# Blockwise causal attention and a max-of-two MLP: w_out asked for one slot later, one k copy on ScalarE, early y copies on VectorE, score bursts further apart, last y tile in three PSUM tiles

## The chip, the cores and the metric

The kernel runs on one core of a Trainium2 chip. The metric is the device time of one execution in microseconds (us). TensorE does the matmuls, VectorE (DVE), ScalarE (ACT) and GpSimd (POOL) the rest; SP only issues transfers. "PEld" is TensorE's weight load.

## The reference, cut to what matters

```python
def _attn_ref(q, k, v):                    # q, k, v: (8, 8, 576, 64) float32
    scores = scale * np.matmul(q, k.transpose(0, 1, 3, 2))
    ...                                    # causal by blocks of 64: block_i >= block_j
    attn = np.exp(scores - max); attn = attn / sum
    return np.matmul(attn, v)

def _moe_ref(x, w1, w2, w_out):            # x: attention output as (4608, 512)
    g = np.maximum(x @ w1, x @ w2)         # w1, w2: 512 x 1024
    return g @ w_out                       # w_out: 1024 x 512
```

## The kernel before

The program is one hand-made schedule. Two heads make a pair, and 32 pairs make 32 "slots": slot s computes the scores and exps of pair s in two bursts, then the attention-times-v matmuls of pair s - 2. The matmuls of the MLP (units "h" for w1 and w2, units "y" for w_out) are strewn between as filler, as soon as their tokens are done. q and k arrive in groups of two pairs: a load on the SP queue, a cast to bfloat16 on GpSimd, 18 small transposes on TensorE and two copies, for q and for k each. v and the weights come through GpSimd's queue, which casts on the way.

```python
def y_unit(i, s):                          # one 128 x 512 tile of the output
    ...
        if f == NFF - 1:
            y = y_pool.tile([P, d_model], FP32, name="y")
            nc.scalar.copy(out=y[:], in_=py[:])
            nc.sync.dma_start(out=out[t0:t0 + P, :], in_=y[:])

def pool_work(s):                          # GpSimd's work of slot s
    g, i = divmod(s, 2)
    if s == 4:
        pass
    elif s == 5:
        load_qk(5, (SP, SP), gated=True)
        cast("q", 4, ((pool, 0, RPP),))
    ...

# before the loop over slots (slot 3)
burst_q1(3)
transposes("k", 2, (dve, dve))()
...
cast("q", 3, ((pool, 0, RPP),))
cast("k", 3, ((pool, 0, RPP),))
load_qk(4, (SP, SP), gated=True)           # q and k group 4, used from slot 6 on
load_wo(0, 4)
load_wo(4, 4)
...
for s in range(HP, NPAIR):                 # slots 4 to 31
    n = fill_of(s)                         # filler of this slot
    burst_a(s)
    n_a = n // 2 if n > 12 else n * 2 // 5
    fill(n_a)                              # filler between the two bursts
    copy_out = t_pair(s)                   # transposes of a later group
    burst_b(s)
    ...
```

The PSUM pool of everything but scores has four buffers, in rotation. "Gated" loads are those whose place in time GpSimd sets: it writes one element of the buffer first.

The softmax here doesn't subtract the row's maximum and nothing guards it: scores larger than these inputs give would overflow.

## Time and profile before

| | before |
|---|---|
| time, median of 3 runs | 291.29 us |
| span of the profiled run | 289.4 us |
| TensorE busy | 280.3 us, 97% |
| VectorE, ScalarE, GpSimd busy | 64%, 48%, 35% |
| transfers from 22 to 48 us | the 16 DMA engines never idle |

Busy shares say that TensorE is the bound. They do not say where it waits, and only there can this change win. The useful reading is a list of gaps between neighbouring matmuls, each with what ended it. The prediction below gives it, with the lines of the timelines and of the chain of waits.

Wherever the kind of matmul changes between full 128-row and half 64-row form, the gap is about 0.095 us more than the steady step. The Trainium skill, "TensorEngine Tiling (Array Packing)", section "Key Properties", says that changing the tiling mode drains TensorE. The traces fit this and give the price. Such gaps are not waits, and no part of this change touches them.

### The profile page before, as it was taken

The numbers are of one execution on the slowest core, as the hardware profiler recorded it, in microseconds if no ns is written. First come the engines' busy times: TensorE is split into PE (matmuls) and PEld (weight loads), VectorE is DVE, ScalarE is ACT, GpSimd is POOL, SyncE is SP. The second block draws the span as 40 slices with busy tenths as digits, with TensorE's granted clock in tenths as the row PEclk, the third lists the DMA queues.
The fourth block names the chain that finished last, engine by engine and source line by source line (L and its number), as shares of the span: only waits on it lengthen the run. The fifth ranks groups of instructions, "written<-read, shape, count | busy, mean of one in ns | idle before, by whom it ended". The sixth has DMA issues, their size and how long they took to land.

```text
span 289.4 us, 7674 instructions
## 1 busy us (share of the span) xinstructions
PE 280.3 (97%) x3200; PEld 145.2 (50%) x3200; DVE 186.2 (64%) x391; ACT 137.8 (48%) x196; POOL 101.2 (35%) x241
## 2 busy tenths in 40 slices
PE   7799989999999999999999999999999999999995
PEld 3356556555554554544454545454454554444443
DVE  6878778548986676666566656567665766545430
ACT  3785755786555555554555554545555110010112
POOL 2978547335635442244334532543111000000000
PEclk9999999999999999999999999999999999999999
DMA  7999999969933792569366593366201011111114
GB/s 265 237 219 276 172 286 216 182 166 165 198 48 134 96 214 49 198 76 228 57 202 70 157 132 99 112 69 72 48 36 39 36 39 72 40 57 52 57 55 145
DMA packets 56083, 36.68 MB, mean 127 GB/s; under 512 B 38768, under 2 KB 43376, under 8 KB 56048
## 3 DMA queue, kind: packets, MB, share of 16 engines
q0 software_dynamic: 41728, 7.87, 33.8%
q1 hardware_dynamic: 13760, 27.60, 28.2%
q10 hardware_dynamic: 560, 0.72, 0.7%
q8 instruction: 25, 0.41, 0.6%
q14 instruction: 10, 0.08, 0.1%
HBM read 34.60 MB, written 9.44 MB: 152 GB/s over the span
## 4 chain that ended last, share of the span: by engine, by line
PE 88%; DMA 4%; issue 2%; DVE 2%; ACT 2%; POOL 1%; ACTq 0%; POOLq 0%; DVEq 0%
PE ps_h L191 41%; PE ps_y L209 21%; PE ps_o L396 12%; PE ps_s L318 8%; DMA vv<-in_v_dram 2%; PE ps_xe L418 2%; DMA qraw<-in_q_dram 2%; PE ps_qT L301 2%; PE ps_kT L301 1%; ACT aT L324 1%; PE ps_w L290 1%; DVE xp L403 1%; POOL vv L130 1%; PE ps_y L226 1%; POOL qn L126 1%
## 5 line engine op out<-in xcount | busy, mean ns | idle before, releaser
L191 PE MATMUL ps_h<-xT,w_sb 128*128 128x512 bf16 (+3 forms) x640 | 140.7, 358 | 0.4 <-DVE kT L308 0.2
L324 ACT ACTIVATE aT<-ps_s 128x1024 bf16<-128x1024 f32 (+3 forms) x128 | 100.1, 832 | 60.4 <-PE ps_s L318 58.5
L191 PEld LDWEIGHTS <-w_sb 128*128 128x128 bf16 x640 | 56.8, 98 | 57.1 <-issue 6.1
L198 DVE CAST h<-ps_h 128x512 bf16<-128x512 f32 (+3 forms) x80 | 50.9, 636 | 43.4 <-PE ps_h L191 41.2
L209 PE MATMUL ps_y<-wo_sb,g 128*128 128x512 bf16 x280 | 69.4, 379 | 0.0
L329 POOL MEMSET aT<- 64x128 bf16 x122 | 22.6, 201 | 110.3 <-ACT aT L324 110.0
L215 ACT COPY y<-ps_y 128x512 f32<-128x512 f32 x35 | 20.5, 587 | 81.8 <-PE ps_y L209 59.3
L200 DVE TENSOR_TENSOR g<-h,ps_h 128x512 bf16<-128x512 bf16 (+3 forms) x80 | 50.6, 632 | 9.9 <-PE ps_h L191 7.6
L396 PEld LDWEIGHTS <-aT 128*128 128x128 bf16 x960 | 34.0, 98 | 14.6 <-DVE xp L403 7.2
L396 PE MATMUL ps_o<-vv,aT 128*128 128x65 bf16 x960 | 40.2, 194 | 0.5 <-DMA vv<-in_v_dram 0.4
L209 PEld LDWEIGHTS <-g 128*128 128x128 bf16 x280 | 25.5, 98 | 27.4 <-issue 3.0
L318 PE MATMUL ps_s<-qT,kT 64*128 64x64 bf16 (+6 forms) x408 | 34.7, 269 | 1.3 <-ACT kT L308 0.7
L130 POOL DMA_DIRECT2D vv<-in_v_dram x40 | 33.7, 849 | 0.0
L403 DVE TENSOR_TENSOR xp<-ps_o,rec 128x256 bf16<-128x256 f32 (+1 forms) x64 | 31.4, 491 | 2.2
L318 PEld LDWEIGHTS <-kT 64*128 64x128 bf16 x408 | 16.2, 94 | 15.4 <-issue 9.7
L402 DVE RECIPROCAL rec<-ps_o 128x4 f32<-128x4 f32 (+1 forms) x64 | 11.8, 185 | 14.6 <-PE ps_o L396 14.5
L126 POOL CAST qn<-qraw 128x1152 bf16<-128x1152 f32 (+1 forms) x15 | 16.5, 1102 | 6.9 <-DMA qraw<-in_q_dram 6.7
L126 POOL CAST kn<-kraw 128x1152 bf16<-128x1152 f32 x15 | 17.2, 1145 | 4.1 <-DMA kraw<-in_k_dram 2.0
L181 POOL COPY g<-g 128x512 bf16<-128x512 bf16 x8 | 4.9, 614 | 37.9 <-DVE g L200 37.8
L308 DVE COPY qT<-ps_qT 128x576 bf16<-128x576 bf16 x18 | 13.5, 757 | 5.5 <-PE ps_qT L301 4.6
L308 DVE COPY kT<-ps_kT 128x576 bf16<-128x576 bf16 x18 | 13.5, 755 | 3.9 <-PE ps_kT L301 2.8
L423 DVE COPY xT<-ps_xe 128x640 bf16<-128x640 bf16 (+2 forms) x18 | 8.2, 453 | 11.9 <-PE ps_xe L418 11.4
(40 smaller groups left out, 110.9 us busy)
## 6 DMA issues: line engine op xcount, KB each, us to landing
qraw<-in_q_dram SPq DMA_DIRECT2D x16, 576.0 KB, 4.5
out_dram<-y SPq DMA_DIRECT2D x35, 256.0 KB, 2.1
kraw<-in_k_dram SPq DMA_DIRECT2D x15, 576.0 KB, 6.3
vv<-in_v_dram POOLq DMA_DIRECT2D x32, 128.0 KB, 5.6
w_sb<-in_moe_w_dram POOLq DMA_DIRECT2D x4, 256.0 KB, 6.5
w_sb<-in_moe_w_dram POOLq DMA_DIRECT2D x2, 512.0 KB, 14.2
wo_sb<-in_moe_w_out_dram POOLq DMA_DIRECT2D x2, 512.0 KB, 16.0
kraw<-in_k_dram ACTq DMA_DIRECT2D x1, 576.0 KB, 5.4
```

What stands on the lines that cost most here:

```text
L126: copy(out=n[:, j0:j1], in_=t[:, j0:j1])
L130: nc.gpsimd.dma_start(out=vv_r[b % NV][:rows, c, :, :D], in_=v[b, :, c * P:c * P + rows, :].rearrange("h p d -> p h d"),)
L191: nc.tensor.matmul(pt[:, :w], w_sb[:, c, f * P:(f + 1) * P], xT[:, c, t0:t0 + w], start=(c == 0), stop=(c == NDM - 1),)
L198: nc.vector.tensor_copy(out=h1[:, :w], in_=pt[:, :w])
L200: nc.vector.tensor_max(g[:, f, m:m + w], h1[:, :w], pt[:, :w])
L209: nc.tensor.matmul(py[:], g[:, f, s * P:(s + 1) * P], wo_sb[:, f, :], start=(f == 0), stop=(f == NFF - 1),)
L308: copies[i](out=t[:, :S].rearrange("q (p j) -> q p j", j=RPP), in_=pts[i].rearrange("q j p -> q p j"),)
L318: nc.tensor.matmul(ps[:m, hh, col:col + w], kT[r, c * P:c * P + m], qT[r, q0:q0 + w], start=True, stop=True,)
L324: nc.scalar.activation(out=aT_r[p % NA][:m, :, a0:a0 + w], in_=ps[:m, :, :w], func=AF.Exp, scale=scale,)
L329: (eng or nc.gpsimd).memset(aT_r[p % NA][BLK:, :, a0:a0 + BLK], 0.0)
L396: nc.tensor.matmul(po[:, gi, hh, :], a[:, hh, a0:a0 + P], vv[:, c, h0 + 2 * hh, :], start=(mm == 0), stop=(mm == n_mm - 1),)
L403: nc.vector.tensor_mul(xp[:, ts[0]:ts[0] + n, :, p % 2], po[:, :, :, :D], rec[:, :n].to_broadcast([P, n, 2, D]),)
```

## The change

Its intent: w_out's megabyte should not compete with the load of q group 4; ScalarE, which has the exps, should not have y copies in front of them; VectorE, busy in slot 3, should give one k copy to ScalarE; the filler of slot 4 should cover the wait for its exp; the two halves of the last tile's copy should not wait for each other.

```diff
--- before.py
+++ after.py
@@ -212,28 +212,24 @@
             )
             if f == NFF - 1:
                 y = y_pool.tile([P, d_model], FP32, name="y")
-                nc.scalar.copy(out=y[:], in_=py[:])
+                (dve if i < 2 else act)(out=y[:], in_=py[:])
                 nc.sync.dma_start(out=out[t0:t0 + P, :], in_=y[:])
             yield
 
     def y_last(i, s):
         g = g_tiles[i]
         t0 = spans[i][0] - carry[i] + s * P
-        w = d_model // 2
-        for h in range(2):
+        for m, w, copy, queue in ((0, 256, act, SP), (256, P, dve, SP), (384, P, act, ACT)):
             py = ps_m.tile([P, w], FP32, name="ps_y", tag="m")
             for f in range(NFF):
                 nc.tensor.matmul(
-                    py[:], g[:, f, s * P:(s + 1) * P], wo_sb[:, f, h * w:(h + 1) * w],
+                    py[:], g[:, f, s * P:(s + 1) * P], wo_sb[:, f, m:m + w],
                     start=(f == 0), stop=(f == NFF - 1),
                 )
                 if f == NFF - 1:
-                    for u, (copy, queue) in enumerate(((act, ACT), (dve, SP))):
-                        m = u * w // 2
-                        y = y_pool.tile([P, w // 2], FP32, name="yl")
-                        copy(out=y[:], in_=py[:, m:m + w // 2])
-                        queue.dma_start(
-                            out=out[t0:t0 + P, h * w + m:h * w + m + w // 2], in_=y[:])
+                    y = y_pool.tile([P, w], FP32, name="yl")
+                    copy(out=y[:], in_=py[:])
+                    queue.dma_start(out=out[t0:t0 + P, m:m + w], in_=y[:])
                 yield
 
 
@@ -247,7 +243,7 @@
         def y(i, s, last=False):
             t0, w = spans[i]
             if last:
-                units.append((y_last(i, s), t0 + w, 0.5, 2 * NFF))
+                units.append((y_last(i, s), t0 + w, 0.333, 3 * NFF))
             else:
                 units.append((y_unit(i, s), t0 + w, 1.0, NFF))
 
@@ -440,7 +436,8 @@
     def pool_work(s):
         g, i = divmod(s, 2)
         if s == 4:
-            pass
+            load_wo(0, 4)
+            load_wo(4, 4)
         elif s == 5:
             load_qk(5, (SP, SP), gated=True)
             cast("q", 4, ((pool, 0, RPP),))
@@ -527,7 +524,7 @@
         load_v(1, c)
     fill(3)
     burst_q1(3)
-    transposes("k", 2, (dve, dve))()
+    transposes("k", 2, (dve, act))()
     av(0, [3, 4])
     fill(3)
     burst_q2(3)
@@ -535,8 +532,6 @@
     cast("q", 3, ((pool, 0, RPP),))
     cast("k", 3, ((pool, 0, RPP),))
     load_qk(4, (SP, SP), gated=True)
-    load_wo(0, 4)
-    load_wo(4, 4)
     fill(3)
     av(1, [3, 4])
     fill(4)
@@ -548,7 +543,7 @@
             x_out(x_due.pop(), 3 if s < HP + 2 else 0)
         n = fill_of(s)
         burst_a(s)
-        n_a = n // 2 if n > 12 else n * 2 // 5
+        n_a = n // 2 if n > 12 else n * 3 // 5
         n_b = n // 6
         fill(n_a)
         copy_out = t_pair(s)
```

## The prediction

> **What bounds the kernel now.** I read the page first, then the gaps between matmuls, then what ended each gap. The page says TensorE is busy for 97% of the span and its clock is fully granted, and the chain of waits agrees:
>
> ```profile
> span 289.4 us, 7674 instructions
> PE 280.3 (97%) x3200; PEld 145.2 (50%) x3200; DVE 186.2 (64%) x391; ACT 137.8 (48%) x196; POOL 101.2 (35%) x241
> ...
> PE 88%; DMA 4%; issue 2%; DVE 2%; ACT 2%; POOL 1%; ACTq 0%; POOLq 0%; DVEq 0%
> ```
>
> So a change that adds no faster matmul can win only where TensorE waits. I looked for those places by subtracting, for each pair of neighbouring matmuls, the steady step of the first kind (0.2155 us for 512 columns, 0.162 for 384, 0.030 for an attention-times-v matmul) from the distance of their starts. A change of matmul kind costs about 0.095 us everywhere; beyond that, from 70 us to 210 us no gap exceeds 0.125 us. The change touches only what lies before 66 us and after 284 us. In those parts the real waits are these. In slot 4: about 0.09 us at 26.7, 0.68 us at 28.9 (scores wait for an exp) and 0.15 us at 31.4. In slot 6: 1.00 us before the transposes of q group 4. From 46.6 to 50.4: about 1.3 us in which VectorE is behind. In slot 9: 0.19 us at 59.1. The large one, in the timelines of TensorE, GpSimd and the SP queue:
>
> ```profile
> 40.12 0.44 PE L301 MATMUL ps_qT<-ident,qn 64*128 64x64 bf16 x18 [0.93 <-POOL qn L126]
> ...
> 30.38 1.50 POOL L144 DMA_DIRECT2D wo_sb<-in_moe_w_out_dram  x2
> 31.92 0.64 POOL L329 MEMSET aT<- 64x128 bf16 x4
> ...
> 38.92 1.14 POOL L126 CAST qn<-qraw 128x1152 bf16<-128x1152 f32 x1 [2.20 <-DMA qraw<-in_q_dram]
> ...
> 30.44 0.37 SPq L116 DMA_DIRECT2D qraw<-in_q_dram  x1
> ```
>
> TensorE waits for a cast, the cast waits for a load of q, and that load was issued at 30.44, 0.06 us after the two w_out loads began to be issued. The view of the transfers, for issues near 30.4 us, gives how long they took:
>
> ```profile
> qraw<-in_q_dram SPq DMA_DIRECT2D x1, 576.0 KB, 8.4
> wo_sb<-in_moe_w_out_dram POOLq DMA_DIRECT2D x1, 512.0 KB, 14.6
> ```
>
> The median load of q takes 4.5 us, this one 8.4. It looks as if w_out were in its way; that is plainly the intent of the first part of the change.
>
> The other two places, in the chain:
>
> ```profile
> 58.88 0.49 ACT y L215
> ...
> 284.48 1.76 PE ps_y L226 x16
> 286.24 0.02 issue
> 286.26 0.28 ACT yl L234
> 286.54 0.02 issue
> 286.56 0.29 DVE yl L234
> ```
>
> In slot 9 a y copy sits behind two exps on ScalarE, and its PSUM buffer is what the next attention matmuls need. At the end, VectorE's copy of the last quarter starts only when ScalarE's has ended, and the last store (1.6 us to landing) is issued after both.
>
> **What the Trainium skill says.** "DMA: Bandwidth & Descriptors", section "Queues, rings and completion order", says each of the 16 engines serves its queues in turn, packet by packet, and takes one queue's work in ring order. The trace agrees: while the q load and w_out run together (37.0 to 39.5 us) each half microsecond has about 45 packets of the SP queue and 40 of GpSimd's; and w_out, issued from 30.38, has its first packet only at 35.5, when nearly all of the v loads issued before it on that queue are through. "PSUM — Partial Sum Buffer", section "PSUM bank collisions raise a hardware error", says two engines may not use one bank's partitions at once, so software orders them; the ScalarE-then-VectorE order of the last tile in the chain shows just that. "VectorE: DVE Perf Modes", "Why PSUM operands drop a tier", says a float32 source in PSUM runs at the base rate; the 128x512 casts here take 691 ns against ScalarE's 587 ns for a y copy.
>
> **Part by part.**
>
> 1. *w_out later.* The order of GpSimd's instructions shows what "one slot" is: the two loads move behind the four masks of slot 4. Those masks took 0.64 us once GpSimd was free, and slot 4's third exp, which the last needs, ends at about 30.5. So the loads start at about 31.0 instead of 30.38: 0.6 us, not the six of a slot. And they stand in their ring behind v packets, which last to about 35.5 on most engines, so the first w_out packet should hardly move. The packet records also show the completion marks of this q load: fifteen of its sixteen came by 37.98, the last at 38.56, and until 39.4 a thin trickle of v packets (about 18 per us, one ring's worth) goes on. I read that as one lagging engine, where v and q alternate and w_out has not begun. Delaying w_out cannot help that engine much. I put the gain at 0.15 us: zero most likely, up to the whole 1.0 us if I misread the laggard. w_out itself landed at 45.0 and 48.5; 0.6 us later is still 3 us before its first use at 52.1.
>
> 2. *k copy on ScalarE* (slot 3) takes 0.71 us off VectorE, which is busy 1.86 of the two microseconds from 24 to 26; ScalarE is idle for 0.79 us there. It lets the x transposes at 27.0 start 0.09 us sooner.
>
> 3. *Bursts further apart* changes one slot only: in slot 4 four h matmuls instead of three stand before the second burst. They fill 0.16 us of the 0.68 us wait for the exp.
>
> Parts 2 and 3 together give 0.25 us, but before 38.9 us, where TensorE stands still for q anyway. The load's time does not depend on them: its issue is set by the k load before it (issued 18.16, 10.9 us to landing, so 29.06; its cast starts at 29.22). They only lengthen the wait from 1.00 to 1.25 us. Worth 0, unless q lands sooner.
>
> 4. *Early y copies on VectorE*: four tiles at about 0.69 us (the 128x512 cast row). The one at 58.76 can now start when its matmuls end, 58.0, because VectorE is idle for 2.8 us before 59.07; the buffer is free at 58.7, before the attention matmuls want it at 59.2. Gain 0.19 us. The other three fall after attention work in slots 8 to 10 with VectorE idle 2.81, 0.69 and 1.81 us around them: free.
>
> 5. *Last tile in three.* Eight matmuls of 256 columns become 16 of 128. From the steps seen (0.110 us for 256, 0.083 for 192) a 128-column one takes about 0.056, so TensorE takes 0.88 + 16 x 0.056 = 1.78 us, 0.02 more. After its end only one copy (0.27 us) remains instead of ScalarE's and VectorE's (0.28 + 0.02 + 0.29). The final store then goes out at 286.58 instead of 286.87. Gain 0.29 - 0.02 = 0.27 us.
>
> Sum: 0.15 + 0 + 0.19 + 0.27 = 0.61 us. 291.29 - 0.6 = 290.7 us.
>
> **Rivals.**
> - *w_out really was what delayed q.* For it: they share engines from 35.5 to 38.9, in which some 250 w_out packets of 97 ns pass, 250 x 97 / 16 = 1.5 us of every engine. Against: ring order keeps w_out where it is, and 0.6 us of delay is little. If true, q lands up to 1 us sooner, and parts 2 and 3 pay as well: 1.0 to 1.25 us more, 289.5.
> - *The wait moves to v.* The last v load of batch 1 lands at 25.6 + 14.6 = 40.2 us and is needed at 41.4. If q came over a microsecond sooner, this would be the next wait; it caps the first rival, not the estimate.
> - *VectorE becomes the bound.* From 46.6 to 50.4 it holds TensorE up, but the y copies begin only at 54.7, after that. If a copy landed before a kT or qT copy it could cost 0.3 us: 291.0.
> - *Later w_out or other packet order makes q or k land later.* GpSimd builds w_out's descriptors just after 31 us, when the k load is being issued on SP (1.35 us there, against 0.42 elsewhere). A shift by half a microsecond either way: 291.3.
>
> **Range and chances.** Copies and tail are firm to about 0.15 us. The q load is the wide term: most likely 0, with a tail to 1.0-1.25 us of gain and a thinner one to 0.5 us of loss. So 290.7, eight in ten from 289.6 to 291.2. 2% is 5.8 us, more than all the waits touched together; faster 0.01, same 0.98, slower 0.01.
>
> **What would show it.** GpSimd's issue of w_out near 31.0, its first packets still near 35.5, and the cast of q still starting between 38.7 and 39.0 with a TensorE wait of 1.0 to 1.3 us before its transposes (step 1 to 3); if the cast starts before 38.5, the ring-order argument is wrong. No gap over 0.1 us before the attention matmuls in slot 9 (step 4). One copy after the last matmul and about 0.29 us less from there to the end (step 5). The middle, 70 to 210 us, must keep its length; a change there would mean I missed something.

## The result, and the profile after

In the same rounds the changed kernel took 290.90 us (median of 4 runs, 290.44 to 290.96) and the kernel before 291.45 us (4 runs, 291.25 to 291.81). The ratio is 0.9976, with a 95% interval of 0.9959 to 0.9994.

Page of the changed kernel, its first lines and the chain by engine:

```profile
span 289.0 us, 7689 instructions
PE 280.2 (97%) x3208; PEld 145.4 (50%) x3208; DVE 187.9 (65%) x393; ACT 136.4 (47%) x193; POOL 101.0 (35%) x241
...
PE 89%; DMA 4%; issue 2%; DVE 2%; POOL 1%; ACT 1%; ACTq 0%; POOLq 0%; DVEq 0%
```

Nothing has changed in kind: eight more matmuls, the same bound. Now the place where TensorE waits for q. Timelines of the changed kernel for TensorE, GpSimd and SP; columns are start, duration, engine, line, operation, and in brackets the idle time before it and what ended that:

```profile
40.02 0.44 PE L297 MATMUL ps_qT<-ident,qn 64*128 64x64 bf16 x18 [0.96 <-POOL qn L126]
...
30.58 0.62 POOL L325 MEMSET aT<- 64x128 bf16 x4
31.15 1.50 POOL L144 DMA_DIRECT2D wo_sb<-in_moe_w_out_dram  x2
...
38.83 1.14 POOL L126 CAST qn<-qraw 128x1152 bf16<-128x1152 f32 x1 [2.23 <-DMA qraw<-in_q_dram]
...
30.51 0.37 SPq L116 DMA_DIRECT2D qraw<-in_q_dram  x1
```

The masks and the w_out loads have changed places, w_out's issue is 0.77 us later (31.15 against 30.38), and the cast of q still begins at 38.83 (38.92 before). The view of the transfers says the same of the load itself:

```profile
qraw<-in_q_dram SPq DMA_DIRECT2D x1, 576.0 KB, 8.3
```

8.3 us to landing, 8.4 before. In slot 9 the y copy is gone from the chain of the changed kernel:

```profile
58.57 0.37 PE ps_kT L297 x18
58.94 0.25 PE ps_s L314 x6
59.19 0.29 PE ps_o L392 x6
```

The attention matmuls follow the scores at once. At the end the chain has one copy where it had two:

```profile
284.23 1.78 PE ps_y L225 x24
286.01 0.02 issue
286.03 0.27 ACT yl L231
```

To see where the time went I cut each profiled run at the same instructions: from the k transposes of group 2 (slot 3) to the moment when TensorE is ready for q group 4; the wait for q there; from q group 5's transposes to q group 6's (holds slot 9); from the last q transposes to the end.

| profiled run | to ready for q4 | wait for q4 | slot 9 stretch | to the end |
|---|---|---|---|---|
| before | 16.37 | 1.00 | 11.33 | 91.39 |
| after | 16.28 | 1.03 | 11.19 | 91.19 |
| difference | -0.09 | +0.03 | -0.14 | -0.20 |

All numbers are in us. The rest agrees: from q group 4's transposes to group 5's 13.15 in both, from group 6's to the last q transposes 133.44 and 133.43. So 0.34 us is won after q has come (0.14 + 0.20), and what is won before is at the mercy of a load.

### The profile page after: what moved, and what is told of

Read it like the earlier page. It is cut to its first block, busy times and chain, and to the rows that moved or that the text cites. A ratio compares the mean times of both kernels' runs of the same rounds, so it can differ in the third digit from the quotient of the medians.

```text
span 289.0 us, 7689 instructions
## 1 busy us (share of the span) xinstructions
PE 280.2 (97%) x3208; PEld 145.4 (50%) x3208; DVE 187.9 (65%) x393; ACT 136.4 (47%) x193; POOL 101.0 (35%) x241
## 4 chain that ended last, share of the span: by engine, by line
PE 89%; DMA 4%; issue 2%; DVE 2%; POOL 1%; ACT 1%; ACTq 0%; POOLq 0%; DVEq 0%
PE ps_h L191 41%; PE ps_y L209 21%; PE ps_o L392 12%; PE ps_s L314 8%; DMA vv<-in_v_dram 2%; PE ps_xe L414 2%; DMA qraw<-in_q_dram 2%; PE ps_qT L297 2%; PE ps_kT L297 2%; PE ps_w L286 1%; ACT aT L320 1%; DVE xp L399 1%; POOL vv L130 1%; PE ps_y L225 1%; POOL qn L126 1%
## 5 line engine op out<-in xcount | busy, mean ns | idle before, releaser
L215 ACT COPY y<-ps_y 128x512 f32<-128x512 f32 x31 | 18.1, 585 | 81.3 <-PE ps_y L209 58.8
L304 DVE COPY kT<-ps_kT 128x576 bf16<-128x576 bf16 x17 | 12.8, 755 | 1.4 <-PE ps_kT L297 0.3
```

The lines of the kernel that those rows point to most:

```text
L304: copies[i](out=t[:, :S].rearrange("q (p j) -> q p j", j=RPP), in_=pts[i].rearrange("q j p -> q p j"),)
```

## The experiments

Twelve kernels in three groups of four, five rounds each; the kernels of a group share the runs of the kernel before, and the second and third group have eleven of these in common. Times are medians. A transfer moves in many small packets. "Marks" are the sixteen increments of a semaphore that make up a landing, read here as one from each of the 16 DMA engines; both are in the trace's records.

### Each part alone

**w_out_only**: the kernel before with this edit.

```diff
-    load_wo(0, 4)            # before the loop
-    load_wo(4, 4)
...
     if s == 4:
-        pass
+        load_wo(0, 4)
+        load_wo(4, 4)
```

> The kernel before with the w_out loads alone moved into slot 4. Theory (ring order and one lagging engine): the issue moves from 30.4 to about 31.1 us, the cast of q group 4 still starts at 38.7 to 39.0, the time is that of before within 0.15 us (ratio 0.9995 to 1.0005). Rival (w_out held q up): the cast starts before 38.4 and the time falls by 0.5 us or more (ratio under 0.9985).

Measured: 291.30 us (6 runs, 290.26 to 291.83) against 291.51 (11 runs, 291.02 to 292.02); ratio 0.9986, interval 0.9970 to 1.0002. In the profile w_out is issued at 30.70, its first packet comes at 35.95 (35.74 before), and the cast of q starts at 38.26, where the theory had 38.7 to 39.0 and the rival less than 38.4: the first half of the rival's sign. But q itself was issued 0.37 us sooner in that run (30.07), and took 8.14 us from issue to landing against 8.43. The clock leans towards a gain but its interval holds zero.

**y_copies_only**: the kernel before with `(dve if i < 2 else act)` for the y copy.

> The kernel before with the first four y copies alone on VectorE. Theory: the 0.19 us wait before the attention matmuls of slot 9 goes and all that follows comes that much sooner, 0.2 us less (ratio about 0.9993). Rival (VectorE becomes the bound in slots 8 to 10): a new gap before a kT or qT copy's reader, no gain or up to 0.3 us lost.

Measured: 291.19 us (6 runs, 291.08 to 291.89), ratio 0.9993, interval 0.9980 to 1.0006. The clock cannot see it, the trace can: the slot 9 stretch is 11.19 us, exactly that of the changed kernel, and no new gap appears in slots 8 to 10.

**last_tile_only**: the kernel before with the new `y_last`.

> The kernel before with the last y tile alone in three PSUM tiles. Theory: from the start of its matmuls to the end of the last copy 2.08 us instead of 2.37, so 0.27 to 0.3 us less in all (ratio about 0.9991). Rival (the last store's landing, not the copy, sets the end, or the 24 smaller matmuls cost more than 0.02 us): under 0.1 us gained.

Measured: 291.50 us (6 runs, 291.02 to 292.13), ratio 1.0001, interval 0.9987 to 1.0014: nothing, by the clock. But in the profiled run the last stretch is 91.16 us, 0.23 less than before, while q group 4 happened to land at 39.51 instead of 38.87 and TensorE waited 1.78 us for it. A part that saves 0.2 us is lost in a load that scatters by more than a microsecond.

**k_and_burst_only**: the kernel before with `(dve, act)` for the k copies and `n * 3 // 5`.

> The kernel before with the k copy on ScalarE and the bursts of slot 4 further apart, nothing else. Theory: the matmuls of slots 4 to 6 run up to 0.25 us sooner, and the wait before the transposes of q group 4 grows by as much; the time is that of before within 0.1 us. Rival (the wait is a chain of compute that moves along): 0.15 to 0.25 us less.

Measured: 291.31 us (6 runs, 291.09 to 292.34), ratio 0.9999, interval 0.9983 to 1.0014. In the profile TensorE is ready for q 16.28 us after the k transposes, 0.09 sooner than before, not 0.25. The wait for q did not grow as expected: it was 0.83 us, because this load took only 8.05 us. The changed kernel's timeline shows where the other 0.16 us went; the first line is a wait in slot 4 that the moved matmul was to fill, the second the next one:

```profile
29.52 0.21 PE L314 MATMUL ps_s<-qT,kT 64*128 64x64 bf16 x2 [0.52 <-ACT aT L320]
...
31.67 0.20 PE L414 MATMUL ps_xe<-ident,xp 64*128 64x64 bf16 x1 [0.22 <-DVE xp L399]
```

The wait for the exp keeps its 0.52 us in this view. The matmul fills a smaller gap just before it, and is then missing after it, where the x transposes wait for VectorE: in the list of gaps that one grows from 0.25 to 0.39 us. A filler that only changes places among several waits of one chain wins nothing.

### What holds q up

**w_out_two_slots**: the changed kernel with w_out issued after q group 5 has been asked for.

```diff
     elif s == 5:
         load_qk(5, (SP, SP), gated=True)
+        load_wo(0, 4)        # and gone from s == 4
+        load_wo(4, 4)
         cast("q", 4, ((pool, 0, RPP),))
```

> The changed kernel with the w_out loads a real slot later still, issued at about 36.7 us, after q group 5 has been asked for. Theory (the last of the sixteen marks of the q load comes from an engine that is busy with v, not with w_out): fifteen marks come sooner, by 37.3, but the sixteenth stays at 38 to 38.6 and the cast at 38.4 to 38.9; the time is that of the changed kernel within 0.3 us, if w_out lands before its first use at 52. Rival (w_out shares its way): the cast starts when GpSimd has issued w_out, at 38.2, with q long landed by 37.5, and 0.6 us or more are won.

Measured: 290.65 us (5 runs, 290.39 to 290.81) against 291.61 (11 runs, 291.05 to 292.06); ratio 0.9968, interval 0.9955 to 0.9981. GpSimd's timeline:

```profile
36.90 1.51 POOL L144 DMA_DIRECT2D wo_sb<-in_moe_w_out_dram  x2 [0.35 <-issue]
38.46 1.14 POOL L126 CAST qn<-qraw 128x1152 bf16<-128x1152 f32 x1
```

That the cast follows the issue at once would fit the rival. The marks decide: w_out's first packet came at 41.02, so nothing of it was on the engines, and q still landed at 38.41, 8.2 us after its issue. The second rival fact failed too, and so did mine: I had expected fifteen marks by 37.3, and the fifteenth came at 38.19 (38.30 before). So w_out is not what slows q on the other fifteen engines either.

**v_later**: the changed kernel with two of the five v loads of batch 1 put behind q.

```diff
     mask_q(2)
-    for c in range(3, NCH):
-        load_v(1, c)
...
     if s == 4:
+        load_v(1, 3)
+        load_v(1, 4)
         load_wo(0, 4)
         load_wo(4, 4)
```

> The changed kernel with the last two v loads of batch 1 (1536 of its 4608 packets) issued in slot 4 just ahead of w_out, not before q group 4. Theory: the lagging engine has fewer v packets ahead of and beside q, so the sixteenth mark comes about 1 us or more sooner and the cast starts before 38.0; the gain is eaten if these v loads then land after 40.5, where the attention matmuls of slot 6 wait for them. Rival (the q load is slow for another reason, such as its own engine or its late start): cast still at 38.7 to 39.0.

Measured: 289.89 us (5 runs, 289.76 to 289.98), ratio 0.9941, interval 0.9929 to 0.9954: by the ratios (0.9941 against 0.9976) a microsecond better than the changed kernel. Transfers of q group 4 and GpSimd's cast of it, in two views:

```profile
qraw<-in_q_dram SPq DMA_DIRECT2D x1, 576.0 KB, 6.0
```

```profile
36.61 1.14 POOL L126 CAST qn<-qraw 128x1152 bf16<-128x1152 f32 x1
```

```profile
38.95 0.43 PE L297 MATMUL ps_qT<-ident,qn 64*128 64x64 bf16 x18
```

The last line is TensorE's: no bracket, no wait. The packet records show it on both sides of the laggard, before q starts to move and while it moves. Before, q is issued at 30.44 and has its first packet at 33.20, 2.8 us later; in the seven profiled runs that have neither the v edit nor the early load, wherever w_out stands, this delay is 2.8 to 3.4 us. In the 2.8 us of the kernel before, 3076 packets of v started and none of SP's queue. With 1536 v packets fewer ahead the delay is 1.6 us (1.4 to 1.8 in the four later kernels with this edit). And after that all sixteen marks come sooner, the fifteenth at 36.29 instead of 38.30. This kernel also issues w_out later, but w_out_two_slots moved w_out further still without this effect. So v was the cause, on every engine and not just one.

**early_q** and **early_q_less_two**: the load of q and k group 4 put before the cast of k group 3; the second also has the k copy and the bursts as they were before.

```diff
     cast("q", 3, ((pool, 0, RPP),))
+    load_qk(4, (SP, SP), gated=True)
     cast("k", 3, ((pool, 0, RPP),))
-    load_qk(4, (SP, SP), gated=True)
```

> The changed kernel with the load of q and k group 4 asked for one cast earlier on GpSimd, about 2.5 us sooner (at 27.9 instead of 30.5 us). Theory: q lands before TensorE needs it, the 1.0 us wait before its transposes goes, and the 0.25 us of the k copy and the bursts is paid out as well: 1.0 to 1.2 us less than the changed kernel (289.8). Rival (the DMA engines are full from 22 to 48 us, so the wait moves): v of batch 1 or k lands after 40.5 and a new wait stands in slot 6; under 0.4 us won.

> The same early load of q, but with the k copy on VectorE and the bursts of slot 4 as they were before. Theory: if the wait for q is gone, these two parts are worth their 0.2 to 0.25 us, so this is that much slower than early_q. Rival (they are worth nothing anywhere): equal to early_q within 0.1 us.

Measured: early_q 290.39 us (6 runs, 289.70 to 291.76), ratio 0.9956, interval 0.9938 to 0.9975; early_q_less_two 289.99 us (5 runs, 289.88 to 290.17), ratio 0.9945, interval 0.9933 to 0.9958. In both profiles the wait for q is gone. The profiled run of early_q lost its gain to another load, in a place that the edit had not reached yet:

```profile
28.26 0.50 PE L191 MATMUL ps_h<-xT,w_sb 128*128 128x384 bf16 x2 [1.55 <-DMA w_sb<-in_moe_w_dram]
```

So this pair cannot be compared by the clock, which even has them in the wrong order. By the trace, early_q_less_two needs 16.37 us from the k transposes to being ready for q, and v_later, which has the two parts, 16.28. With the wait out of the way they are worth 0.09 us, not 0 and not 0.25.

### The parts again without the wait for q

**quiet_base**: the kernel before with only the two v loads moved, to just ahead of w_out. **quiet_y** and **quiet_last_tile**: the same with one part of the change.

> The kernel before with nothing changed but the last two v loads of batch 1, issued just ahead of w_out and behind q group 4. Theory (these v packets hold q up, and the wait for q is both a loss and the source of the scatter): no wait before the transposes of q group 4, about 290.3 to 290.5 us, and runs within 0.4 us of each other instead of 1.0. Rival (the five parts of the change are needed for the gain of v_later): 291 or more.

> quiet_base with the four y copies on VectorE. Theory: 0.14 us less than quiet_base, as the stretch from q group 4 to the last transposes showed (157.78 against 157.92 us). Rival: 0, the earlier gain was noise.

> quiet_base with the last y tile in three PSUM tiles. Theory: 0.3 us less than quiet_base, as the stretch from the last transposes to the end of the profile showed (88.52 against 88.81 us, last landing included). Rival (the first clock reading, 291.5 against 291.5, was right): 0.

Measured against 291.57 us (12 runs, 291.02 to 292.06): quiet_base 290.41 us (5 runs, 290.30 to 290.99, ratio 0.9959, interval 0.9945 to 0.9973), quiet_y 290.76 us (5 runs, 290.22 to 291.19, ratio 0.9972, interval 0.9957 to 0.9987), quiet_last_tile 290.10 us (4 runs, 290.01 to 290.28, ratio 0.9950, interval 0.9935 to 0.9964).

quiet_base hits its time and has no wait for q, so v alone is worth about 1.2 us without any part of the change. It was not as quiet as hoped: its runs lie 0.69 us apart, not 0.4. quiet_y came out slower by the clock, with intervals that overlap. In its profile, and in that of quiet_base (second line), TensorE waits in slot 6:

```profile
41.47 0.71 PE L396 MATMUL ps_o<-vv,aT 128*128 128x65 bf16 x13 [0.46 <-DMA vv<-in_v_dram]
...
41.55 0.34 PE L396 MATMUL ps_o<-vv,aT 128*128 128x65 bf16 x6 [0.23 <-DMA vv<-in_v_dram]
```

The last v load landed at 41.85 and 41.51 (40.56 in v_later), and the attention matmuls waited: from q group 4's to group 5's transposes quiet_y and quiet_base took 13.92 and 13.74 us, against 13.15 in the kernels before and after. The wait of the one load had become the wait of the other. It makes quiet_base, too, a poor measure for the clock. The slot 9 stretch of quiet_y is 11.19 us against 11.33 in quiet_base, so the 0.14 us are there again. quiet_last_tile's stretch to the end is 91.16 us against 91.38, and its clock is 0.3 us under that of quiet_base, which leans the same way, though the intervals overlap. My expectation for it holds an error: 88.52 and 88.81 us run to the end of the last copy, not to the landing. To the end of the program the difference is 0.20 to 0.22.

**v_later_act**: v_later with the casts of two h units in slot 7 on ScalarE.

```diff
-                        nc.vector.tensor_copy(out=h1[:, :w], in_=pt[:, :w])
+                        (act if i == 1 and f in (5, 6) else dve)(out=h1[:, :w], in_=pt[:, :w])
```

> v_later with two of span 1's casts of h (f 5 and 6) on ScalarE, which is idle then, in the stretch where VectorE holds TensorE up (about 46 to 50 us, 1.3 us of gaps). Theory: the gaps after 48 us (0.14 + 0.20 + 0.15) shrink, 0.2 to 0.4 us less than v_later, 289.6. Rival (the max that follows on VectorE waits just as long): 0 to 0.1 us.

Measured: 289.48 us (6 runs, 289.29 to 290.11), ratio 0.9933, interval 0.9918 to 0.9949. This beats both kernels: it is 1.4 us under the changed one by medians that come from different rounds (290.90 and 289.48), 1.25 by the ratios. Against v_later the intervals overlap, and the trace must decide. VectorE of v_later, then ScalarE of v_later_act, for the same two casts:

```profile
47.93 0.56 DVE L399 TENSOR_TENSOR xp<-ps_o,rec 128x384 bf16<-128x384 f32 x1
48.41 0.35 DVE L198 CAST h<-ps_h 128x192 bf16<-128x192 f32 x1
48.86 0.35 DVE L200 TENSOR_TENSOR g<-h,ps_h 128x192 bf16<-128x192 bf16 x1
49.13 0.35 DVE L198 CAST h<-ps_h 128x192 bf16<-128x192 f32 x1
```

```profile
48.08 0.32 ACT L198 CAST h<-ps_h 128x192 bf16<-128x192 f32 x1 [0.81 <-PE ps_h L191]
48.74 0.32 ACT L198 CAST h<-ps_h 128x192 bf16<-128x192 f32 x1 [0.34 <-PE ps_h L191]
```

VectorE's row has no idle time between its instructions: it is the bound there. ScalarE was free and waited for the matmuls. The three gaps after 48 us are gone from the list, and the distance from q group 4's to q group 7's transposes fell from 36.17 to 35.61 us, 0.56 less and more than expected.

## Why the prediction was right or wrong

The total was right: 290.9 us against 290.7, inside the range. In part that is luck: the traces show where 0.34 us of the gain comes from (0.46 foreseen), and the rest is not traced to a cause; the prediction's 0.15 us for w_out was a hedge between zero and 1.0. The steps:

**1, w_out later.** The issue at 31.0 (31.15 measured), the cast still between 38.7 and 39.0 (38.83) and the wait of 1.0 to 1.3 us (1.03) came as written. The first packets did not stay near 35.5: they came at 36.50, 0.76 us after those of the kernel before (35.74), as much later as the issue. Four profiled runs with w_out in its old place spread from 35.47 to 36.28, so this decides nothing. (The prediction's times of packets and marks are some 0.3 us early, counted from another zero than its timelines: the fifteenth and last mark at 37.98 and 38.56 are 38.30 and 38.87 there. No step rests on it.) The first rival, that w_out was what delayed q by the microsecond, fell with w_out_two_slots. But the reason I gave was only half right. "I read that as one lagging engine, where v and q alternate and w_out has not begun": a last mark that trails the others is often there, yet what makes q late is the v traffic ahead of it on all engines, as v_later showed. The failed step is that I looked at the end of the load, where the trickle was, and not at its start, where 2.8 us passed before its first packet. The turn-taking of queues that the prediction quotes fits the packets from 37.0 to 39.5 us; in those 2.8 us it does not, since v and the last of w1 and w2 moved and none of q. Why SP's queue got no turn there is not shown.

Of its size: the changed kernel, w_out_only and w_out_two_slots are 0.70, 0.41 and 0.93 us faster than before by ratio (one minus the ratio, times about 291). If the 0.34 us of the other parts is taken off where they are present, 0.36, 0.41 and 0.59 us remain, against my 0.15. Only the last of the three is clearly more than nothing by its interval. But they come from three separate sets of rounds, and weighted by their intervals they average 0.48 us, give or take 0.25 (an estimate from these numbers): a few tenths are likelier than zero. The marks hint at a path. In these three runs and the four with w_out in its old place the fifteenth mark came 7.7 to 8.1 us after q's issue; the last one trailed it by 0.16 to 0.41 us in the three and by 0.17 to 1.56 in the four. Against it speaks quiet_base, where q had landed (37.46) before w_out's first packet (37.54) and the last mark still trailed by 0.66 us. With one profile of each kernel, what moving w_out is worth, and how, stays open.

**2 and 3, k copy and bursts.** "Worth 0, unless q lands sooner" fits: 0.9999 alone, though with an interval of some 0.45 us either way the clock cannot tell 0 from 0.25. The size of what waits behind was wrong: part 2's 0.09 us was right, but part 3's "They fill 0.16 us of the 0.68 us wait for the exp" measured 0, because another wait on VectorE follows in the same slot.

**4, early y copies.** Right in mechanism: the copy started at 57.96 and took 0.69 us, as worked out, and the other three were free. The term was mis-sized by a little: 0.14 instead of 0.19 us. The gap itself shrank by the full 0.19; about 0.04 of it came back 0.5 us later, where a short gap of the kind seen in slot 8 (0.04 us) had been hidden before.

**5, last tile.** Right in mechanism, 0.20 instead of 0.27 us. TensorE took 1.78 us, as written, and the last copy ended 0.30 us sooner. Of that, 0.03 was lost in the store (1.61 us from issue to landing on ScalarE's queue against 1.58 on SP's) and 0.07 after the landing: SP checks the queues one after another at the end, and with ScalarE's store as the last it had two more to check instead of one.

**The rivals.** "The wait moves to v" did not happen in the changed kernel, since q did not come sooner, but it is what quiet_base and quiet_y ran into. VectorE did not become the bound in slots 8 to 10. Nor did k land later: k group 4 came at 41.68 us, 41.88 before.

**The range.** Taking the q load as the wide term was right, and it is also what makes the clock coarse: the kernel before scatters over 1.0 us (12 runs), v_later over 0.2 (5 runs).

## What to carry to other kernels

When a transfer is late, look at when its first packet moves as well as when its last one lands: what shares its time is not always what holds it up, and here it was mainly the traffic issued before it. Filler and copies moved ahead of a wait for a transfer are not won, and one place further on they may meet the next wait of the same chain. When the parts of a change are smaller than the scatter of one load, cut the profiles at common instructions and compare stretches; in all profiled runs that have or lack the part, the slot 9 stretch and the last one repeated to 0.03 us that way, while the clock had the order of two pairs wrong.

## What the Trainium skill lacked or had wrong

- "DMA: Bandwidth & Descriptors", section "Latency and other measured facts", gives about 600 ns to the first byte of a load issued from SP. No figure is given for a load that starts behind a full queue of small packets: here 2.8 to 3.4 us with all of v ahead, 1.4 to 1.8 us in the five runs with 1536 of its 4608 packets moved behind.
- "TensorEngine Tiling (Array Packing)", section "Key Properties", says that a change of tiling mode drains TensorE, without a price. It was about 0.095 us at each change between 128-row and 64-row matmuls in these traces.
- "Runtime: NRT & Kernel Launch", section "The ~15µs preamble/postamble breakdown", lists a closing barrier among the runtime's stages around a kernel. No page gives the time from the last landing to the end of a program, or what it depends on. From the last landing to the last instruction it was 0.97 us before and 1.04 us after, where the queue that landed last stood one place earlier in SP's checks.
